# Metering TensorE's side work by a token bucket, and starting attention on the first block of keys

## The chip, the cores and the metric

One core of one Trainium2 chip. The metric is the device time of one execution of the program in microseconds (us). The kernel's time is a median of several runs, and one execution is also profiled: its trace is what the text reads. The core's engines are TensorE (PE in the profile: matmuls, with weight loads shown apart as PEld), VectorE (DVE), ScalarE (ACT), GpSimd (POOL) and SyncE (SP). Each runs its own queue of instructions in the order written; they meet at semaphores.

## The reference

Two equal layers over x of 2048 tokens by 512, in bfloat16, and each layer does two steps:

```python
x = x + A(layernorm(x))     # attention: 32 heads of 16, all 2048 keys, no mask
x = x + B(layernorm(x))     # (gelu(x @ w_gate) * (x @ w_up)) @ w_down, 1792 wide

def A(x):
    q, k, v = split(x @ wqkv)                       # each 32 heads x 2048 x 16
    p = softmax(q @ k.T * 16 ** -0.5)
    return merge_heads(p @ v) @ wo
```

Both layers use the same weights. The layer norm has no scale and no shift.

## The kernel before

All activations stay on the chip. `X` holds the residual as 16 tiles of 128 tokens in float32; `XNT` holds the normalised x, transposed; `KT` the keys, `VP` the values with a column of ones, `WQM` the query weights spread out so that four heads fill the array's row groups with zeros between.

**Slots.** The attention of a layer is cut into 32 units: four blocks of 512 queries (`qb`) times eight groups of four heads (`g`). A unit has 32 slots: 16 tiles of 128 keys (`kt`) times two pairs of heads (`hp`). A slot (`a_slot`) is two score matmuls on TensorE side by side (line 608), and one exponential of 128 x 1024 on ScalarE (line 613). Both layers together have 2048 slots. The scores go round three pairs of PSUM banks, so TensorE can be up to two slots ahead of ScalarE. After a lag of three slots the second slot of a pair is followed by `pv` (line 626): four matmuls side by side that add into bank 7. At the end of a unit VectorE copies bank 7 out (line 453), and after four units the sums' reciprocals are sent through DRAM and multiplied in on GpSimd (line 437, `AT`).

**Side work.** Everything else that TensorE does is put between slots by a planner written in Python; its decisions fix each engine's order of instructions. There are two sources. `prep` is a list of projections with gates: keys and values of each pair of head groups (`kproj`, `vproj`; lines 343 and 358 copy them out) and the query of each unit (`qproj`, copied out by line 337). `posts` holds a generator per block of queries (`post`): it waits for the block's last unit, then gives the four out-projections (into `X`, line 473), the layer norm (`ln_tiles`: statistics on VectorE, lines 284 and 285; scaling on GpSimd, lines 289 to 295), ten slots later four transposes (`transpose_tile`, lines 308 and 312), then the gate projections with their gelus in one burst (`g_slot`, lines 577 and 583), 14 up-projections (multiplied into `HT` by line 513) and 4 x 7 pieces of the down-projection (line 521, copied out by 537 or 532). For all layers but the last it ends with the layer norm for the next layer. All this side work but the gate burst uses one PSUM bank, `misc.banks = [6]`.

Each step has a nominal cost: 216 ns for a matmul of 512 columns, so 864 for a query, key or up-projection, 1024 for values, 1728 for an out-projection, 432 for a piece of the down-projection, 224 for a transposed tile. In every slot, side work is given out as long as the sum spent in that slot is under `BUDGET`, 520. So one projection, or two pieces of the down-projection, go into every slot while there is any.

`force` makes a missing query, key or value at once; where its block has not yet passed through `post`, it drains `posts`, with seven PSUM banks. That happens at the layer boundary: in slot 24 of layer two, whose keys of block 3 need the end of layer one's block 3. The post of the last block runs after the last slot in the same way.

**Head.** Loads of `X` go out from GpSimd's queue in four pieces of 512 tokens (issued at 1.3, 2.3, 3.1 and 3.8 us), converted to float32 on the way; weights go out from SP's queue: the keys', queries' and values', then, after ScalarE has cleared `WOP`, eight pieces of wo, then gate, up and down. VectorE clears `WQM` and spreads the query weights into it (8 copies, line 263). GpSimd clears and fills some tiles (lines 253 to 278). Then, for each of the four blocks: layer norm, four transposes; after block 0 also its keys, the first query and its values. The slots begin after the fourth block.

The planner's loop before the change:

```python
spent = 0.0
...                                   # slot: force q and k, a_slot, run_pv, flush_norm
while spent < BUDGET:
    c = prep_try()
    if c is None:
        break
    spent += c
while spent < BUDGET and posts:
    c = next(posts[0], "end")
    ...
    spent += c
```

Of the kernel before, what the change touches and what calls it, by code (L numbers as in the profile page):

```python
# [9 lines left out]
ALU = mybir.AluOpType  # L10
ACTF = mybir.ActivationFunctionType
# [140 lines left out]
def _emit_fast(nc, es, x_in, wqkv, wo, wg, wu, wd, out, n_rep=2):  # L152
# [5 lines left out]
    NCK = D // 128  # L158
    NG = 2 * NCK
    NFT = F // 128  # L160
    NTT = S // 128
    NQB = S // 512
# [62 lines left out]
    class Ring:  # L225
# [4 lines left out]
        def next(self):  # L230
            self.pos += 1
            return self.banks[self.pos % len(self.banks)]
# [3 lines left out]
    def dma(eng, grp, dst, src, r=(), w=(), serial=False):  # L236
        if grp not in sch.groups:
            sch.add_dma_group(grp, serial=serial)
        sch.op(eng, lambda e: e.dma_start(dst, src), r=r, w=w, grp=grp)  # L239

    def pe(fn, r, w):
        sch.op("pe", fn, r=r, w=w)


    wq_src = wqkv.rearrange("(a p) n -> p a n", p=128)
    for b in range(NQB):
        dma("pool", "ldx%d" % b, X[:, 4 * b:4 * b + 4, :],
            x_in[0, 512 * b:512 * (b + 1), :].rearrange("(a p) c -> p a c", p=128),
            w=[("X", 4 * b + i) for i in range(4)])
# [5 lines left out]
    sch.op("pool", lambda e: e.affine_select(IDN[:], ONB[:], [[1, 128]], ALU.is_equal, 0.0,  # L255
                                              base=0, channel_multiplier=-1),
           r=[("ONB",)], w=[("IDN",)])
    sch.op("dve", lambda e: e.memzero(WQM[:].rearrange("p a b c -> p (a b c)")), w=[("WQM",)])
    for c in range(NCK):
        for p in range(2):  # L260
            dst = AP(WQM, (2 * c + p) * 128 + 16 * p, [[NCK * NG * 128, 128], [NG * 128, NCK], [32, 4], [1, 16]])
            src = AP(HT, 128 * c + 16 * p, [[NFT * 512, 128], [D, NCK], [32, 4], [1, 16]])
            sch.op("dve", lambda e, dst=dst, src=src: e.tensor_copy(dst, src), r=HTALL + [("WQM",)], w=[("WQM",)])
    sch.op("dve", lambda e: e.memset(PS[:, 7, :], 0.0), w=[BK[7]])
    sch.op("act", lambda e: e.memzero(WOP[:].rearrange("p a b -> p (a b)")), w=[("WOP", j, p) for j in range(4) for p in range(2)])
    for j in range(4):
        for p in range(2):
            src = AP(wo.tensor, wo.offset + (32 * j + 16 * p) * D, [[D, 16], [128 * D, NCK], [1, D]])
            dst = AP(WOP, 32 * j * NG * D + p * D, [[NG * D, 16], [2 * D, NCK], [1, D]])
            dma("sp", "ldw_o%d%d" % (j, p), dst, src, w=[("WOP", j, p)])  # L270
    dma("sp", "ldw_g", WG[:], wg.rearrange("(a p) n -> p a n", p=128), w=[("WG",)])
    dma("sp", "ldw_u", WU[:], wu.rearrange("(a p) n -> p a n", p=128), w=[("WU",)])
    dma("sp", "ldw_d", WD[:], wd.rearrange("(a p) n -> p a n", p=128), w=[("WD",)])
    sch.op("pool", lambda e: e.memset(AP(VP, 16, [[NKT * H * VW, 128], [VW, NKT * H]]), 1.0), w=[("VPONE",)])
    sch.op("pool", lambda e: e.memset(RB[:], 0.0), w=[("RB", i, j) for i in range(2) for j in range(4)])
    sch.op("pool", lambda e: e.memset(OKL[:], 1.0), w=[("OKL",)])
# [1 line left out]
    sch.op("pool", lambda e: e.memset(LT[:], 1.0), w=[("LT", i, j) for i in range(HB) for j in range(4)])  # L278


    def ln_tiles(tts, check=False):
        n = len(tts)
        for i, tt in enumerate(tts):
            sch.op("dve", lambda e, i=i, tt=tt: e.bn_stats(ST[:, i, :], X[:, tt, :]), r=[("X", tt)], w=[("ST", i)])
            sch.op("dve", lambda e, i=i: e.bn_aggr(MV[:, i, :], ST[:, i, :]), r=[("ST", i)], w=[("MV", i)])
        mvk = [("MV", i) for i in range(n)]
        mean = AP(MV, 0, [[8, 128], [2, n]])
        var = AP(MV, 1, [[8, 128], [2, n]])
        sch.op("pool", lambda e: e.tensor_scalar(LNS[:, 0, 0:n], var, LN_EPS, None, op0=ALU.add), r=mvk, w=[("LNS",)])
        sch.op("pool", lambda e: e.tensor_tensor(LNS[:, 1, 0:n], LNS[:, 0, 0:n], CM05[:, 0:n], op=ALU.pow),  # L290
               r=[("LNS",), ("CM05",)], w=[("LNS",)])
        sch.op("pool", lambda e: e.tensor_scalar(LNS[:, 2, 0:n], mean, -1.0, None, op0=ALU.mult),
               r=mvk + [("LNS",)], w=[("LNS",)])
        for i, tt in enumerate(tts):
            sch.op("pool", lambda e, i=i, tt=tt: e.tensor_scalar(  # L295
                XN[:, i, :], X[:, tt, :], LNS[:, 2, i:i + 1], LNS[:, 1, i:i + 1], op0=ALU.add, op1=ALU.mult),
                r=[("X", tt), ("LNS",)], w=[("XN", i)])
# [5 lines left out]
    def transpose_tile(i, tt):  # L303
        b = misc.next()

        def fn(e):
            for ck in range(NCK):
                ins = e.transpose(bankbf(b)[:, ck * 128:(ck + 1) * 128], XN[:, i, ck * 128:(ck + 1) * 128], IDN[:, :])  # L308
            return ins

        pe(fn, [("XN", i), ("IDN",)], [BK[b]])
        sch.op("dve", lambda e: e.tensor_copy(XNT[:, :, tt * 128:(tt + 1) * 128],  # L312
                                              bankbf(b)[:, 0:NCK * 128].rearrange("p (a b) -> p a b", a=NCK)),
               r=[BK[b]], w=[("XNT", tt)])
        return 56.0 * NCK

    def mm512(pairs, rkeys, evac, cols=512):
# [12 lines left out]
    def xk(b):  # L330
        return [("XNT", 4 * b + i) for i in range(4)]

    def qproj(u, slot):
        qb, g = u // NG, u % NG
        return mm512([(WQM[:, ck, g, :], XNT[:, ck, 512 * qb:512 * (qb + 1)]) for ck in range(NCK)],
                     xk(qb) + [("WQM",)],
                     lambda b: sch.op("dve", lambda e: e.tensor_copy(Q[:, slot, :], bank(b)),  # L337
                                      r=[BK[b]], w=[("Q", slot)]))

# [294 lines left out]
    posts = []  # L634
# [14 lines left out]
            misc.banks = [6]  # L649


    misc.banks = list(range(7))
    for b in range(NQB):
        ln_tiles([4 * b + i for i in range(4)])
        for i in range(4):
            transpose_tile(i, 4 * b + i)
        have.add(("xnt", 0, b))
        if b == 0:
            for _ in range(3):
                prep_try()  # L660
    misc.banks = [6]

    seqs = [(layer, u, kt, hp) for layer in range(n_rep) for u in range(NU) for kt in range(NKT) for hp in range(2)]
    LAG = 3
    pend = []
    nxt = 0
    BUDGET = 520.0

    def run_pv(limit):
        while pend and pend[0][0] <= limit:  # L670
# [12 lines left out]
    while nxt < len(seqs) or pend:  # L683
        step = state["step"]
        if state["gslots"] is not None and nxt < len(seqs):
            qb = state["gslots"]
            for pair in range(NFT // 2):
                g_slot(qb, pair)
            state["gslots"] = None
        spent = 0.0  # L690
# [12 lines left out]
        flush_norm(step)  # L703
        while spent < BUDGET:
            c = prep_try()
            if c is None:
                break
            spent += c
        while spent < BUDGET and posts:
            c = next(posts[0], "end")  # L710
            if c == "end":
                posts.pop(0)
                continue
            if c is None:
                break
            spent += c
        state["step"] += 1
    flush_norm()
    misc.banks = list(range(7))
# [862 lines left out]
```

## Time and profile before

| | us |
|---|---|
| median of 3 runs (2504.36 to 2505.81) | 2504.52 |
| the profiled execution | 2506.37 |
| its span, first to last instruction | 2504.6 |
| ScalarE busy | 1993.2 |
| TensorE matmuls busy | 2159.2 |
| start of the first exponential | 52.74 |
| granted TensorE clock, mean of the span | 0.659 |

In the profile's rows an instruction group has its line, engine, operation, tile written and tiles read, shape and count, then busy time, mean ns of one, and the idle time of its engine before it with what ended that. In a timeline a row gives start and length in us, and in square brackets the idle time before it with what ended it. A row of windows gives the stretch, its length, and for each engine the busy time with the count of instructions; then the granted TensorE clock (1.00 is full), the share of DMA and GB/s. A matmul's end is modelled, so the distance between starts is the better measure.

### The profile page before, as it was taken

How to read it: one execution, taken by the hardware profiler on the slowest of the kernel's cores; microseconds unless marked ns; L12 is line 12 of the kernel's file. 1: busy time of each engine (PE TensorE's matmuls, PEld its weight loads, DVE VectorE, ACT ScalarE, POOL GpSimd, SP SyncE). 2: the span in 40 equal slices, each digit the busy share in tenths (PEclk: the TensorE clock that was granted, in tenths of full speed). 3: DMA queues.
4: the chain of work that ended last, by engine and by line, in shares of the span. 5: the costliest groups of instructions: out<-in, count | busy, mean ns of one | idle time of the engine just before them, and what ended most of it. 6: DMA issues, size and time to landing. Idle time of an engine off the chain costs nothing.

```text
span 2504.6 us, 25781 instructions
## 1 busy us (share of the span) xinstructions
PE 2159.2 (86%) x10945; PEld 537.1 (21%) x10945; DVE 361.0 (14%) x634; ACT 1993.2 (80%) x2121; POOL 160.9 (6%) x192
## 2 busy tenths in 40 slices
PE   3899889888889888898788888889988998889968
PEld 1321112111221112212132211221112111221113
DVE  4210012100120002100132100210012000120003
ACT  1689976999769996899727899679986899769971
POOL 4000010000100000000100000100000000100000
PEclk7855569555795558756588655785568655695558
DMA  7000000000000000000000000000000000000000
GB/s 189 1 1 10 1 10 1 1 10 1 10 1 10 1 10 1 1 10 1 10 1 1 1 10 4 7 9 10 1 10 3 7 10 1 10 9 6 5 10 10
DMA packets 21147, 25.07 MB, mean 10 GB/s; under 512 B 5920, under 2 KB 13856, under 8 KB 21024
## 3 DMA queue, kind: packets, MB, share of 16 engines
q1 hardware_dynamic: 18912, 19.16, 3.0%
q0 software_dynamic: 2112, 4.19, 0.6%
q8 instruction: 87, 1.43, 0.2%
q14 instruction: 36, 0.29, 0.0%
HBM read 18.09 MB, written 2.62 MB: 8 GB/s over the span
## 4 chain that ended last, share of the span: by engine, by line
ACT 54%; PE 31%; DVE 8%; DMA 3%; POOL 2%; SPq 2%; issue 1%; POOLq 0%; DVEq 0%
ACT fPT L613 54%; PE fPS L323 13%; PE fPS L577 4%; PE fPS L521 4%; PE fPS L608 4%; DVE fHT L513 2%; PE fPS L626 2%; SPq L239 2%; PE fPS L353 2%; DMA fRB<-rscr 1%; PE fPS L308 1%; POOL fXN L295 1%; POOL fAT L437 1%; DVE fVP L358 1%; DVE fKT L343 1%
## 5 line engine op out<-in xcount | busy, mean ns | idle before, releaser
L613 ACT ACTIVATE fPT<-fPS 128x1024 bf16<-128x1024 f32 x2048 | 1913.4, 1184 | 390.8 <-PE fPS L608 389.3
L608 PE MATMUL fPS<-fQ,fKT 32*128 32x512 bf16 x4096 | 1102.1, 553 | 172.5 <-ACT fPT L613 163.4
L626 PE MATMUL fPS<-fPT,fVP 128*17 128x512 bf16 x4096 | 573.1, 550 | 1.4 <-ACT fPT L613 1.4
L608 PEld LDWEIGHTS fPS<-fQ,fKT 32*128 32x128 bf16 x4096 | 198.7, 97 | 1064.0 <-ACT fPT L613 984.9
L453 DVE COPY fOS<-fPS 128x512 f32<-128x512 f32 x64 | 44.3, 692 | 1361.6 <-PE fPS L626 1361.6
L437 POOL TENSOR_TENSOR fAT<-fOS,fRB 128x512 bf16<-128x512 f32 x64 | 81.0, 1265 | 1874.9 <-DMA fRB<-rscr 1874.9
L626 PEld LDWEIGHTS fPS<-fPT,fVP 128*17 128x17 bf16 x4096 | 101.1, 90 | 400.0 <-issue 395.8
L323 PE MATMUL fPS<-fXNT,fWU 128*128 128x512 bf16 x448 | 111.6, 381 | 23.2 <-DVE fHT L513 18.1
L583 ACT ACTIVATE fHT<-fPS 128x1024 bf16<-128x1024 f32 x56 | 57.4, 1024 | 92.3 <-PE fPS L577 92.3
L521 PE MATMUL fPS<-fWD,fHT 128*128 128x512 bf16 x448 | 113.7, 381 | 13.1 <-DVE fXN L532 4.7
L323 PE MATMUL fPS<-fXNT,fWQM 128*128 128x512 bf16 x256 | 111.8, 587 | 4.3 <-DVE fX L537 1.4
L577 PE MATMUL fPS<-fXNT,fWG 128*128 128x512 bf16 x448 | 110.4, 412 | 0.8 <-DVE fXNT L312 0.5
L513 DVE TENSOR_TENSOR fHT<-fPS,fHT 128x512 bf16<-128x512 f32 x112 | 77.5, 692 | 216.5 <-PE fPS L323 216.3
L323 PE MATMUL fPS<-fWOP,fAT 128*128 128x512 bf16 x256 | 74.8, 447 | 37.5 <-POOL fAT L437 31.3
L308 PE MATMUL fPS<-fIDN,fXN 128*128 128x128 bf16 x256 | 38.9, 307 | 70.1 <-POOL fXN L295 56.3
L577 PEld LDWEIGHTS fPS<-fXNT,fWG 128*128 128x128 bf16 x448 | 46.3, 105 | 63.9 <-issue 18.8
L337 DVE CAST fQ<-fPS 128x512 bf16<-128x512 f32 x64 | 44.3, 692 | 71.0 <-PE fPS L323 71.0
L323 PEld LDWEIGHTS fPS<-fXNT,fWU 128*128 128x128 bf16 x448 | 37.0, 98 | 80.6 <-DVE fHT L513 46.1
L521 PEld LDWEIGHTS fPS<-fWD,fHT 128*128 128x128 bf16 x448 | 36.0, 98 | 69.1 <-issue 16.3
L323 PE MATMUL fPS<-fXNT,fWK 128*128 128x512 bf16 x128 | 40.3, 446 | 9.8 <-DVE fVP L358 5.9
L295 POOL TENSOR_SCALAR fXN<-fX,fLNS 128x512 bf16<-128x512 f32 x64 | 48.3, 770 | 1.7
L473 DVE TENSOR_TENSOR fX<-fPS,fX 128x512 f32<-128x512 f32 x32 | 22.1, 692 | 181.3 <-PE fPS L323 181.3
(45 smaller groups left out, 391.0 us busy)
## 6 DMA issues: line engine op xcount, KB each, us to landing
fRB<-rscr SPq DMA_DIRECT2D x256, 32.0 KB, 1.8
fX<-in_A_x_dram POOLq DMA_DIRECT2D x4, 1024.0 KB, 17.2
fLT<-fOS SPq DMA_DIRECT2D x256, 2.0 KB
out_dram<-fXN SPq DMA_DIRECT2D x16, 128.0 KB, 1.7
fWG<-in_B_w_gate_dram SPq DMA_DIRECT2D x1, 1792.0 KB, 19.3
fWU<-in_B_w_up_dram SPq DMA_DIRECT2D x1, 1792.0 KB, 24.6
fWD<-in_B_w_down_dram SPq DMA_DIRECT2D x1, 1792.0 KB, 29.2
fWK<-in_A_wqkv_dram SPq DMA_DIRECT2D x1, 512.0 KB, 4.3
```

The lines of the kernel that those rows point to most:

```text
L239: sch.op(eng, lambda e: e.dma_start(dst, src), r=r, w=w, grp=grp)
L295: sch.op("pool", lambda e, i=i, tt=tt: e.tensor_scalar(XN[:, i, :], X[:, tt, :], LNS[:, 2, i:i + 1], LNS[:, 1, i:i + 1], op0=ALU.add, op1= ...
L308: ins = e.transpose(bankbf(b)[:, ck * 128:(ck + 1) * 128], XN[:, i, ck * 128:(ck + 1) * 128], IDN[:, :])
L323: ins = e.matmul(bank(b)[:, 0:cols], lhsT=l, rhs=r_, start=(i == 0), stop=(i == n - 1))
L437: sch.op("pool", lambda e, g=g, slot=slot, os_=os_: e.tensor_tensor(AT[:, g, :], OS[:, os_, :], RB[:, slot, :], op=ALU.mult), r=[("OS", os ...
L513: lambda b, ft=ft: sch.op("dve", lambda e: e.tensor_tensor(HT[:, ft, :], bank(b), HT[:, ft, :], op=ALU.mult), r=[BK[b], ("HT", ft)], w=[(" ...
L521: ins = e.matmul(bank(b)[:, 0:D], lhsT=HT[:, ft, i * 128:(i + 1) * 128], rhs=WD[:, ft, :], start=(ft == 0), stop=(ft == NFT - 1))
L577: ins = e.matmul(bank(2 * s + jj), lhsT=WG[:, ck, ft * 128:(ft + 1) * 128], rhs=XNT[:, ck, xs], start=(ck == 0), stop=(ck == NCK - 1))
L583: sch.op("act", lambda e: e.activation(HT[:, 2 * pair:2 * pair + 2, :], PS[:, 2 * s:2 * s + 2, :], ACTF.Gelu_apprx_tanh), r=bks, w=[("HT", ...
L608: ins = e.matmul(bank(2 * s + jj), lhsT=KT[32 * j:32 * j + 32, c, kt * 128:(kt + 1) * 128], rhs=Q[32 * j:32 * j + 32, qs, :], start=True, ...
L613: sch.op("act", lambda e: e.activation(PT[:, p, :].rearrange("p (a b) -> p a b", a=2), PS[:, 2 * s:2 * s + 2, :], ACTF.Exp, scale=SCALE), ...
L626: ins = e.matmul(PS[32 * j:32 * j + VW, 7, :], lhsT=VP[:, kt, h, :], rhs=PT[:, ps[j // 2], (j % 2) * 512:(j % 2 + 1) * 512], start=(kt == ...
```

## The change

- **Bucket.** A slot no longer has a budget of its own. Tokens are added at 420 a slot up to 600, and side work is given out while the tokens are above zero, so that a costly piece is paid back in the slots after it.
- **Head.** Block 0 of `X` is loaded in four tiles. Before the first slot only block 0 is normalised and transposed (copied out by ScalarE instead of VectorE) and its keys and the first query made; block 1's layer norm stands before that in VectorE's and GpSimd's queues. A generator, `head`, is put first into `posts`: it gives the transposes of blocks 1, 2 and 3 from slots 5, 13 and 21 on, each after the layer norm of the next block. Odd blocks are normalised into `AT`, which is free then, instead of `XN`.
- **Setup.** Clearing `WQM` and spreading it go from VectorE to ScalarE, clearing `WOP` from ScalarE to GpSimd. Each part of `WQM` has a key of its own. The loads of gate, up and down wait until all of `X` has landed.

```diff
-    for b in range(NQB):
+    for t in range(4):
+        dma("pool", "ldx0_%d" % t, X[:, t, :], x_in[0, 128 * t:128 * (t + 1), :], w=[("X", t)])
+    for b in range(1, NQB):
         dma("pool", "ldx%d" % b, X[:, 4 * b:4 * b + 4, :],
...
-    sch.op("dve", lambda e: e.memzero(WQM[:].rearrange("p a b c -> p (a b c)")), w=[("WQM",)])
+    sch.op("act", lambda e: e.memzero(WQM[:].rearrange("p a b c -> p (a b c)")), w=[("WQM",)])
...
-            sch.op("dve", lambda e, dst=dst, src=src: e.tensor_copy(dst, src), r=HTALL + [("WQM",)], w=[("WQM",)])
+            sch.op("act", lambda e, dst=dst, src=src: e.activation(dst, src, ACTF.Copy), r=HTALL + [("WQM",)],
+                   w=[("WQMx", c, p)])
...
-    sch.op("act", lambda e: e.memzero(WOP[:].rearrange("p a b -> p (a b)")), w=[...])
+    sch.op("pool", lambda e: e.memzero(WOP[:].rearrange("p a b -> p (a b)")), w=[...])
...
-    dma("sp", "ldw_g", WG[:], wg.rearrange("(a p) n -> p a n", p=128), w=[("WG",)])
+    dma("sp", "ldw_g", WG[:], wg.rearrange("(a p) n -> p a n", p=128), r=[("X", NTT - 1)], w=[("WG",)])
...                                                    # the same for ldw_u and ldw_d
+        if eng == "act":
+            sch.op("act", lambda e: e.activation(dst, src, ACTF.Copy), r=[BK[b]], w=[("XNT", tt)])
+        else:
+            sch.op("dve", lambda e: e.tensor_copy(dst, src), r=[BK[b]], w=[("XNT", tt)])
...
+    def head():
+        def ln(b):
+            ln_tiles([4 * b + i for i in range(4)], alt=bool(b % 2) and NG >= 4)
+
+        ln(0)
+        for b in range(NQB):
+            if b + 1 < NQB:
+                ln(b + 1)
+            for i in range(4):
+                transpose_tile(i, 4 * b + i, alt=bool(b % 2) and NG >= 4, eng="act" if b == 0 else "dve")
+            have.add(("xnt", 0, b))
+            yield None
+            while not state["drain"] and state["step"] < 8 * b + 5:
+                yield None
+
+    posts.append(head())
     misc.banks = list(range(7))
-    for b in range(NQB):
-        ln_tiles([4 * b + i for i in range(4)])
-        for i in range(4):
-            transpose_tile(i, 4 * b + i)
-        have.add(("xnt", 0, b))
-        if b == 0:
-            for _ in range(3):
-                prep_try()
+    next(posts[0])
+    prep_try()
+    prep_try()
     misc.banks = [6]
...
-    BUDGET = 520.0
+    RATE, CAP = 420.0, 600.0
+    tokens = 0.0
...
-        while spent < BUDGET:
+        tokens = min(CAP, tokens + RATE)
+        while tokens > 0:
             c = prep_try()
             if c is None:
                 break
-            spent += c
-        while spent < BUDGET and posts:
+            tokens -= c
+        while tokens > 0 and posts:
             c = next(posts[0], "end")
...
-            spent += c
+            tokens -= c
```

More of the change, by code (lines that the diff above doesn't have):

```diff
@@ L262, in _emit_fast @@
             src = AP(HT, 128 * c + 16 * p, [[NFT * 512, 128], [D, NCK], [32, 4], [1, 16]])
-            sch.op("dve", lambda e, dst=dst, src=src: e.tensor_copy(dst, src), r=HTALL + [("WQM",)], w=[("WQM",)])
+            sch.op("act", lambda e, dst=dst, src=src: e.activation(dst, src, ACTF.Copy), r=HTALL + [("WQM",)],
+                   w=[("WQMx", c, p)])
     sch.op("dve", lambda e: e.memset(PS[:, 7, :], 0.0), w=[BK[7]])
-    sch.op("act", lambda e: e.memzero(WOP[:].rearrange("p a b -> p (a b)")), w=[("WOP", j, p) for j in range(4) for p in range(2)])
+    sch.op("pool", lambda e: e.memzero(WOP[:].rearrange("p a b -> p (a b)")), w=[("WOP", j, p) for j in range(4) for p in range(2)])
     for j in range(4):
@@ L270, in _emit_fast @@
             dma("sp", "ldw_o%d%d" % (j, p), dst, src, w=[("WOP", j, p)])
-    dma("sp", "ldw_g", WG[:], wg.rearrange("(a p) n -> p a n", p=128), w=[("WG",)])
-    dma("sp", "ldw_u", WU[:], wu.rearrange("(a p) n -> p a n", p=128), w=[("WU",)])
-    dma("sp", "ldw_d", WD[:], wd.rearrange("(a p) n -> p a n", p=128), w=[("WD",)])
+    dma("sp", "ldw_g", WG[:], wg.rearrange("(a p) n -> p a n", p=128), r=[("X", NTT - 1)], w=[("WG",)])
+    dma("sp", "ldw_u", WU[:], wu.rearrange("(a p) n -> p a n", p=128), r=[("X", NTT - 1)], w=[("WU",)])
+    dma("sp", "ldw_d", WD[:], wd.rearrange("(a p) n -> p a n", p=128), r=[("X", NTT - 1)], w=[("WD",)])
     sch.op("pool", lambda e: e.memset(AP(VP, 16, [[NKT * H * VW, 128], [VW, NKT * H]]), 1.0), w=[("VPONE",)])
@@ L278, in _emit_fast, with xn, xnkey, ln_tiles @@
     sch.op("pool", lambda e: e.memset(LT[:], 1.0), w=[("LT", i, j) for i in range(HB) for j in range(4)])
-    def ln_tiles(tts, check=False):
+    def xn(i, alt):
+        return AT[:, i, :] if alt else XN[:, i, :]
+    def xnkey(i, alt):
+        return ("AT", i) if alt else ("XN", i)
+    def ln_tiles(tts, check=False, alt=False):
         n = len(tts)
@@ L295, in ln_tiles @@
             sch.op("pool", lambda e, i=i, tt=tt: e.tensor_scalar(
-                XN[:, i, :], X[:, tt, :], LNS[:, 2, i:i + 1], LNS[:, 1, i:i + 1], op0=ALU.add, op1=ALU.mult),
-                r=[("X", tt), ("LNS",)], w=[("XN", i)])
+                xn(i, alt), X[:, tt, :], LNS[:, 2, i:i + 1], LNS[:, 1, i:i + 1], op0=ALU.add, op1=ALU.mult),
+                r=[("X", tt), ("LNS",)], w=[xnkey(i, alt)])
         if check:
@@ L301, in ln_tiles, with transpose_tile @@
                    r=mvk + [("OKV",)], w=[("OKV",)])
-    def transpose_tile(i, tt):
+    def transpose_tile(i, tt, alt=False, eng="dve"):
         b = misc.next()
@@ L307, in fn @@
             for ck in range(NCK):
-                ins = e.transpose(bankbf(b)[:, ck * 128:(ck + 1) * 128], XN[:, i, ck * 128:(ck + 1) * 128], IDN[:, :])
+                ins = e.transpose(bankbf(b)[:, ck * 128:(ck + 1) * 128], xn(i, alt)[:, ck * 128:(ck + 1) * 128], IDN[:, :])
             return ins
[L311 to L314, printed above, removed]
+        pe(fn, [xnkey(i, alt), ("IDN",)], [BK[b]])
+        dst = XNT[:, :, tt * 128:(tt + 1) * 128]
+        src = bankbf(b)[:, 0:NCK * 128].rearrange("p (a b) -> p a b", a=NCK)
+        if eng == "act":
+            sch.op("act", lambda e: e.activation(dst, src, ACTF.Copy), r=[BK[b]], w=[("XNT", tt)])
+        else:
+            sch.op("dve", lambda e: e.tensor_copy(dst, src), r=[BK[b]], w=[("XNT", tt)])
         return 56.0 * NCK
@@ L335, in qproj @@
         return mm512([(WQM[:, ck, g, :], XNT[:, ck, 512 * qb:512 * (qb + 1)]) for ck in range(NCK)],
-                     xk(qb) + [("WQM",)],
+                     xk(qb) + [("WQMx", g // 2, g % 2)],
                      lambda b: sch.op("dve", lambda e: e.tensor_copy(Q[:, slot, :], bank(b)),
@@ L689, in _emit_fast @@
             state["gslots"] = None
-        spent = 0.0
         if nxt < len(seqs):
```

## The prediction

> **What bounds the kernel now.** I read the page's first table, then the chain of waits and the costliest groups.
>
> ```profile
> span 2504.6 us, 25781 instructions
> PE 2159.2 (86%) x10945; PEld 537.1 (21%) x10945; DVE 361.0 (14%) x634; ACT 1993.2 (80%) x2121; POOL 160.9 (6%) x192
> ...
> ACT 54%; PE 31%; DVE 8%; DMA 3%; POOL 2%; SPq 2%; issue 1%; POOLq 0%; DVEq 0%
> ...
> L613 ACT ACTIVATE fPT<-fPS 128x1024 bf16<-128x1024 f32 x2048 | 1913.4, 1184 | 390.8 <-PE fPS L608 389.3
> ```
>
> The chain lies on ScalarE (ACT) for 54%: the 2048 exponentials of line 613. Before them ACT is idle 390.8 us, nearly all of it waiting for the scores of line 608. Where nothing but attention runs, ACT does not wait; the timeline of a unit without side work gives its pace, and windows cut at the starts of exponentials show the pace with side work beside it.
>
> ```profile
> 52.74 1.02 ACT L613 ACTIVATE fPT<-fPS 128x1024 bf16<-128x1024 f32 x1 [48.75 <-PE fPS L608]
> ...
> 2047.41 17.52 ACT L613 ACTIVATE fPT<-fPS 128x1024 bf16<-128x1024 f32 x19 [0.85 <-PE fPS L608]
> ...
> core 0: us, PE busy (x) PEld busy (x) DVE busy (x) ACT busy (x) POOL busy (x), PEclk, DMA share, GB/s
> 394.28:417.33 23.05, 19.36 (x102) 5.70 (x100) 8.62 (x13) 14.12 (x14) 0.00 (x0) 1.00 0.00 1
> 417.33:440.32 22.99, 20.81 (x112) 6.15 (x112) 3.46 (x6) 14.34 (x14) 0.00 (x0) 1.00 0.00 1
> ...
> sum 276.23, PE 240.98 PEld 71.10 DVE 72.50 ACT 170.78 POOL 0.00; mean PE 20.08 PEld 5.92 DVE 6.04 ACT 14.23 POOL 0.00
> ...
> 52.74:83.11 30.37, 25.53 (x208) 11.90 (x207) 10.72 (x16) 16.39 (x16) 0.00 (x0) 0.93 0.00 1
> ...
> 1118.51:1122.25 3.74, 3.54 (x18) 0.84 (x18) 0.84 (x2) 2.05 (x2) 0.00 (x0) 0.50 0.03 6
> ...
> sum 137.99, PE 118.73 PEld 54.13 DVE 46.77 ACT 74.12 POOL 0.00; mean PE 16.96 PEld 7.73 DVE 6.68 ACT 10.59 POOL 0.00
> ...
> ...
> sum 80.06, PE 66.89 PEld 22.36 DVE 14.38 ACT 25.74 POOL 5.79; mean PE 11.15 PEld 3.73 DVE 2.40 ACT 4.29 POOL 0.97
> ...
> 1242.38:1306.18 63.80, 47.41 (x218) 20.89 (x218) 24.04 (x47) 10.76 (x10) 9.06 (x14) 0.84 0.00 0
> ```
>
> Undisturbed, nineteen exponentials take 17.52 us, and a single one lasts 1.02 (the first at 52.74), so they follow each other every (17.52 − 1.02) / 18 = 0.917 us. What a stretch takes beyond 0.917 us a slot I call its excess. The up-projection of one block is 14 slots in 23.05 us, 10.2 us of excess; the down-projection is 14 slots in 22.99. Six blocks run so beside attention; their twelve stretches (the first two shown, then the sum) are 168 slots in 276.23 us, an excess of 122 us, 61 each. The seven stretches of key and value projections (first and fourth shown, then their sum) hold 73 slots in 137.99 us: 71 us. The out-projections, four slots in each of six blocks, take 80.06 us (the sum shown): 58 us. The other costs, the head, the gate bursts, the layer boundary and the tail, have other causes. So 251 us are lost because a side unit (four full matmuls, 864 ns by the planner) goes into every slot.
>
> Why a slot with a unit takes 1.83 us is in the timeline of an up-projection and of a down-projection:
>
> ```profile
> 409.72 0.69 DVE L513 TENSOR_TENSOR fHT<-fPS,fHT 128x512 bf16<-128x512 f32 x1 [1.13 <-PE fPS L323]
> 410.47 1.04 PE L323 MATMUL fPS<-fXNT,fWU 128*128 128x512 bf16 x4 [0.47 <-DVE fHT L513]
> 411.44 0.39 PE L608 MATMUL fPS<-fQ,fKT 32*128 32x512 bf16 x2
> ...
> 434.84 0.60 PE L521 MATMUL fPS<-fWD,fHT 128*128 128x512 bf16 x2 [0.79 <-DVE fX L537]
> 435.37 0.39 PE L608 MATMUL fPS<-fQ,fKT 32*128 32x512 bf16 x2
> 435.69 0.39 PE L626 MATMUL fPS<-fPT,fVP 128*17 128x512 bf16 x4
> 436.02 1.04 PE L521 MATMUL fPS<-fWD,fHT 128*128 128x512 bf16 x4
> ```
>
> The unit holds TensorE 0.97 us (410.47 to 411.44), then VectorE empties the only side bank (0.69 us), and the next unit, with the next scores behind it in TensorE's queue, waits for that (0.47). At full clock one slot's scores take 0.32 us (435.37 to 435.69), a pair's PV 0.33, or 0.16 a slot, and two down matmuls 0.53 (434.84 to 435.37). At half clock the same steps are:
>
> ```profile
> 337.27 0.60 PE L608 MATMUL fPS<-fQ,fKT 32*128 32x512 bf16 x2 [0.52 <-ACT fPT L613]
> 337.80 0.61 PE L626 MATMUL fPS<-fPT,fVP 128*17 128x512 bf16 x4
> 338.34 0.60 PE L608 MATMUL fPS<-fQ,fKT 32*128 32x512 bf16 x2
> ...
> 370.23 1.89 PE L323 MATMUL fPS<-fXNT,fWQM 128*128 128x512 bf16 x4
> 372.05 0.61 PE L608 MATMUL fPS<-fQ,fKT 32*128 32x512 bf16 x2
> ```
>
> Scores 0.53, PV 0.27 a slot, a unit 1.82.
>
> **The change, part by part.** *The bucket.* It adds 420 a slot, so a unit of 864 goes out every 864 / 420 = 2.06 slots and a down piece of 432 nearly every slot; work beyond that slips to later slots. A block's side work by the planner's costs, 4 × 1728 + 14 × 864 + 28 × 432 + 8 × 224 = 32,896, then needs 78 slots (at 420) instead of 38 (at 864), of the 256 that a block lasts, so nothing is late but at the layer boundary (below).
>
> Up-projection: TensorE needs 2.06 × 0.48 + 0.97 = 1.96 us a unit, ACT 2.06 × 0.917 = 1.89. TensorE binds by 0.07 us; scores run up to two slots ahead, which evens out the lumps. 84 units × 0.07 = 6; I take 8 instead of 61 (bounds 0 and 61): −53 us.
>
> Down-projection: 1.03 × 0.48 + 0.53 = 1.02 against 0.94, 0.08 for each of 168 pieces, 13 us; at each of 24 tile changes the next piece waits for VectorE, 0.79 less the scores and PV now between, 0.3, 7 us. 20 instead of 61 (bounds 7 and 61): −41 us.
>
> Keys and values: 62 units. These bursts begin at half clock, where a unit costs 2.06 × 0.80 + 1.82 − 1.89 = 1.58 us. I let two units of each of six bursts run so (19 us) and 50 at 0.1: 24 instead of 71 (bounds 5 and 98): −47 us.
>
> Out-projection (eight matmuls, 1728, so every 4.1 slots): at full clock 1.90 + 4.1 × 0.48 = 3.87 against 3.76, next to nothing; at half 3.57 + 4.1 × 0.80 − 3.76 = 3.1. The first of each block stays at half clock and waits for POOL's normalised tile (2.09):
>
> ```profile
> 349.67 3.57 PE L323 MATMUL fPS<-fWOP,fAT 128*128 128x512 bf16 x8 [2.09 <-POOL fAT L437]
> 356.71 1.90 PE L323 MATMUL fPS<-fWOP,fAT 128*128 128x512 bf16 x8
> ```
>
> That is 5.2 a block and nearly nothing for the rest: 32 instead of 58 (bounds 13 and 87): −26 us.
>
> Q projections lie mostly in attention without other side work, one a unit, and stay; some fall into the longer metered stretches: −5 (bounds 0 and −12). The gate bursts are emitted whole, as before: 0. At the layer boundary slot 24 of the next layer forces what is left; two out-projections that ran in slots then fall into that drain, and pay about what they paid: 0.
>
> *The head.*
>
> ```profile
> 6.99 1.25 POOL L275 MEMSET fRB<- 128x1024 f32 x1
> 14.31 0.24 POOL L289 TENSOR_SCALAR fLNS<-fMV 128x4 f32<-128x4 f32 x1 [5.75 <-DVE fMV L285]
> 23.36 0.69 DVE L337 CAST fQ<-fPS 128x512 bf16<-128x512 f32 x1 [0.41 <-PE fPS L323]
> ...
> DMA to landing us min/median/max: 9.0/17.2/26.8
> ```
>
> Block 0's query is cast by 24.05; the first exponential starts at 52.74, as its row showed, because three more blocks are normalised and transposed first. After the change it could start 0.65 us behind the cast, at 24.7. POOL's setup gets longer: the WOP clearing (twice RB's columns, 2.5 us) and three more DMA issues (0 to 2.4) move its end from 8.56 (14.31 less the 5.75 of waiting) to between 11.1 and 13.5, still ahead of 14.31; VectorE loses the WQM copies to ACT, which is idle, and starts its statistics when the tiles land, by 10.3 (issue at 1.3 plus 9.0). So 14.31 moves up by 1.6 or so: first exponential at 23.2. The casts of K and Q now stand behind block 1's statistics on VectorE; were its rows to land 17.2 us after an issue at 2.3, plus 3.4 us of statistics, it would be 25.4 (the other end). −29.5 us.
>
> What it costs: the transposes of blocks 1 to 3 now stand in front of scores, on one side bank: four at 1.12 us (374.03 after 372.90 in the next rows) make 4.5 us, less the two slots' lead. Three of them left ACT idle 2.62 us here. Block by block 3 us, +9 (bounds 3 and 14).
>
> ```profile
> 372.90 0.61 PE L308 MATMUL fPS<-fIDN,fXN 128*128 128x128 bf16 x4 [0.25 <-DVE fQ L337]
> 374.03 0.61 PE L308 MATMUL fPS<-fIDN,fXN 128*128 128x128 bf16 x4 [0.52 <-DVE fXNT L312]
> ...
> 376.34 1.02 ACT L613 ACTIVATE fPT<-fPS 128x1024 bf16<-128x1024 f32 x1 [2.62 <-PE fPS L608]
> ```
>
> The gate, up and down weights now wait on SP for all of X; nothing else stands there until the first unit ends, and they are first read some 270 us on: 0.
>
> Sum: −53 − 41 − 47 − 26 − 5 − 29.5 + 9 = −192.5. The profiled execution took 2506.37 around its span of 2504.6; against the median of 2504.52 I get 2312.
>
> **Does the clock hold?** This decides most. Windows of 3.4 us around a Q projection, and in an up-projection:
>
> ```profile
> 268.30:271.70 3.40, 3.27 (x14) 0.74 (x14) 0.96 (x2) 2.82 (x4) 0.00 (x0) 0.50 0.00 1
> 271.70:275.10 3.40, 2.20 (x20) 0.57 (x16) 0.42 (x1) 3.15 (x4) 0.00 (x0) 0.99 0.01 2
> 275.10:278.50 3.40, 2.96 (x16) 0.50 (x14) 0.00 (x0) 3.40 (x5) 0.00 (x0) 0.51 0.00 0
> ...
> 402.00:405.40 3.40, 2.79 (x16) 0.81 (x15) 1.38 (x2) 1.85 (x2) 0.00 (x0) 1.00 0.00 0
> ```
>
> One unit lifts the granted clock for the next window; a window of attention alone drops it, although TensorE reads busy for 2.96 of its 3.40 us. Metered, a unit comes each 1.9 us instead of each 1.83 and the scores between double, so a window holds as much dense work as the one at 402, which stayed at 1.00. In the row at 410.47 TensorE idled 0.47 us before the unit, and the clock stayed full. The Trainium skill ("TensorE: Matmul & The Clock Gate", section "A second HAM failure mode: psum-queue depth-cycling") speaks against the change: short idle times between groups of matmuls, it says, make the clock swing between half and full. The trace does not agree so far, by that 0.47.
>
> **The rivals.** *Clock lost* (slower): thinned work does not keep the clock. All at half is U 133, D 168 × 0.79 = 133, K and V 98, out-projection 87: 451 where the sum has 84, +367, 2679. It decides from 192.5 / 367 = 52% of the metered work at half clock. For it: attention alone runs at 0.50. Against: the window at 402. 0.04.
>
> *Clock swings*: half of the metered work at half clock, by the idle times that the wider spacing leaves between units: +183, 2495. For it: the clock changes from one 3.4 us window to the next around 271.70. Against: the row at 410.47 and 23 us of up-projection at 1.00. 0.04. This is the skill's section named above.
>
> *Half clock where a burst starts cold*: keys, values and out-projections never lift it, up and down, behind the gate burst, do: +74 + 55, 2441. For it: the two projections at 1118.51 ran at 0.50 throughout. 0.10.
>
> *TensorE is the bound anyway* (the change doesn't do what it says): spread or not, each unit costs the same, and only the head is won, 2484. For it: PE reads 86% busy. Against: 0.48 + 0.97 us of need in a slot of 1.83. 0.04.
>
> *All of it hides*: U 0, D 7, K and V 5, out-projection 13, so 59 less, 2253. 0.13.
>
> **How the numbers follow.** Forecast 0.63, its own range 2280 to 2360; 0.02 for what I do not see. The range takes in the hidden case and the lower part of the cold-burst case: 2250 to 2400, about 0.8. A change of 0.2% (5 us) is about what can be told from none. Faster 0.63 + 0.13 + 0.10 + 0.04 + 0.04 = 0.94, same 0.02, slower 0.04.
>
> **What would show it.** Right: first exponential at 23 to 25.5 us; up-projection units in about 29 slots of some 28 us at clock 1.00; down pieces at about 1.02 us a slot; line 613's idle time down from 390.8 to some 200. Wrong: PEclk below 0.8 in those stretches, exponentials 1.3 us or more apart beside side work, or a drain at the boundary (the row at 1242.38) much over 63.8 us.

## The result, and the profile after

The changed kernel takes 2275.31 us (median of 4 runs, 2274.16 to 2277.6) against 2505.16 for the kernel before in the same session: a ratio of 0.9084, interval 0.9068 to 0.9099. The forecast was 2312 in a range of 2250 to 2400. The time fell by 230 us where 192.5 were forecast, and half of the difference stands in one term of the sum, the queries.

The page of the changed kernel, beside the lines shown of the one before (the exponentials are line 625 now, the scores 620):

```profile
span 2274.6 us, 25800 instructions
PE 2003.7 (88%) x10945; PEld 518.6 (23%) x10945; DVE 353.9 (16%) x621; ACT 1981.6 (87%) x2133; POOL 164.0 (7%) x196
...
ACT 54%; PE 33%; DVE 5%; DMA 3%; POOL 2%; SPq 2%; issue 1%; POOLq 0%; DVEq 0%
...
L625 ACT ACTIVATE fPT<-fPS 128x1024 bf16<-128x1024 f32 x2048 | 1896.9, 1192 | 157.5 <-PE fPS L620 153.2
```

ScalarE's busy time hardly moved (1993.2 to 1981.6); its waiting before exponentials fell from 390.8 to 157.5 us, which is the difference between the two spans, 230.0 us, to within a few us.

Windows of the same stages, cut at starts of exponentials: an up-projection (29 slots), a down-projection (31), the sum of all twelve such stretches, and the drain at the layer boundary. Then ScalarE's timeline at the head and in an up-projection:

```profile
352.73:379.58 26.85, 25.47 (x174) 7.80 (x174) 10.02 (x16) 26.85 (x30) 0.00 (x0) 1.00 0.00 1
380.50:411.78 31.28, 30.39 (x187) 7.76 (x186) 3.78 (x6) 29.53 (x32) 0.00 (x0) 1.00 0.01 1
...
sum 348.78, PE 335.17 PEld 93.35 DVE 82.78 ACT 338.24 POOL 0.00; mean PE 27.93 PEld 7.78 DVE 6.90 ACT 28.19 POOL 0.00
...
1110.36:1177.65 67.29, 51.32 (x233) 22.36 (x231) 25.05 (x48) 10.76 (x11) 9.06 (x14) 0.85 0.00 0
...
22.75 1.02 ACT L625 ACTIVATE fPT<-fPS 128x1024 bf16<-128x1024 f32 x1 [4.82 <-PE fPS L620]
...
359.07 9.62 ACT L625 ACTIVATE fPT<-fPS 128x1024 bf16<-128x1024 f32 x10
```

In the up-projection ScalarE is busy for all of its 26.85 us: 14 side units now lie beside 29 exponentials without a wait, at clock 1.00. The twelve stretches hold 360 slots in 348.78 us, 18.7 us over 0.917 a slot; before they held 168 slots and 122 us of excess. The first exponential starts at 22.75.

To sort all the excess, I put each interval between the starts of two exponentials down to the side work that stands between their scores in TensorE's queue, less 0.917 us:

| term, us | before | after | difference | forecast |
|---|---|---|---|---|
| first exponential | 52.7 | 22.7 | −30 | −29.5 |
| transposes of blocks 1 to 3 among the slots | 0 | 6.3 | +6 | +9 |
| up-projection, 84 units | 61.3 | 1.3 | −60 | −53 |
| down-projection, 168 pieces | 60.9 | 14.0 | −47 | −41 |
| keys and values | 65.5 | 19.4 | −46 | −47 |
| out-projections, with the boundary's | 68.5 | 40.6 | −28 | −26 |
| queries | 76.7 | 52.5 | −24 | −5 |
| gate bursts, other transposes, pure slots, tail | | | −1 | 0 |

(After, 3.5 us of the out-projections' 40.6 are the longer drain: two of them joined it. Beside attention they cost 37.0.)

### The profile page after: what moved, and what is told of

Its sections match the earlier page's. It is cut to its first block, busy times and chain, and to the rows that moved or that the text cites. A ratio compares the mean times of both kernels' runs of the same rounds, so it can differ in the third digit from the quotient of the medians.

```text
span 2274.6 us, 25800 instructions
## 1 busy us (share of the span) xinstructions
PE 2003.7 (88%) x10945; PEld 518.6 (23%) x10945; DVE 353.9 (16%) x621; ACT 1981.6 (87%) x2133; POOL 164.0 (7%) x196
## 3 DMA queue, kind: packets, MB, share of 16 engines
q0 software_dynamic: 2160, 4.19, 0.8%
## 4 chain that ended last, share of the span: by engine, by line
ACT 54%; PE 33%; DVE 5%; DMA 3%; POOL 2%; SPq 2%; issue 1%; POOLq 0%; DVEq 0%
ACT fPT L625 54%; PE fPS L335 11%; PE fPS L620 7%; PE fPS L533 5%; PE fPS L589 5%; PE fPS L638 4%; SPq L239 2%; DVE fHT L525 1%; DMA fRB<-rscr 1%; PE fPS L317 1%; POOL fAT L449 1%; DMA rscr<-fRT 1%; DMA fLT<-fOS 1%; DVE fXNT L326 1%; DVE fQ L349 1%
## 5 line engine op out<-in xcount | busy, mean ns | idle before, releaser
L625 ACT ACTIVATE fPT<-fPS 128x1024 bf16<-128x1024 f32 x2048 | 1896.9, 1192 | 157.5 <-PE fPS L620 153.2
L620 PE MATMUL fPS<-fQ,fKT 32*128 32x512 bf16 x4096 | 997.1, 518 | 159.4 <-ACT fPT L625 149.8
L638 PE MATMUL fPS<-fPT,fVP 128*17 128x512 bf16 x4096 | 536.7, 514 | 4.5 <-DVE fOS L465 2.8
L620 PEld LDWEIGHTS fPS<-fQ,fKT 32*128 32x128 bf16 x4096 | 189.7, 96 | 965.9 <-ACT fPT L625 840.5
L533 PE MATMUL fPS<-fWD,fHT 128*128 128x512 bf16 x448 | 126.2, 383 | 5.3 <-DVE fX L549 1.4
L335 PE MATMUL fPS<-fXNT,fWQM 128*128 128x512 bf16 x256 | 98.7, 527 | 0.9
L317 PE MATMUL fPS<-fIDN,fXN 128*128 128x128 bf16 x224 | 33.6, 304 | 47.0 <-POOL fXN L304 34.4
L293 DVE BATCH_NORM_STATS2 fST<-fX 128x6 f32<-128x512 f32 x64 | 42.7, 667 | 8.3 <-DMA fX<-in_A_x_dram 8.3
L533 PEld LDWEIGHTS fPS<-fWD,fHT 128*128 128x128 bf16 x448 | 30.1, 97 | 58.2 <-issue 32.7
L335 PEld LDWEIGHTS fPS<-fWOP,fAT 128*128 128x128 bf16 x256 | 25.9, 110 | 73.7 <-issue 35.1
```

What stands on the lines that cost most here:

```text
L317: ins = e.transpose(bankbf(b)[:, ck * 128:(ck + 1) * 128], xn(i, alt)[:, ck * 128:(ck + 1) * 128], IDN[:, :])
L335: ins = e.matmul(bank(b)[:, 0:cols], lhsT=l, rhs=r_, start=(i == 0), stop=(i == n - 1))
L533: ins = e.matmul(bank(b)[:, 0:D], lhsT=HT[:, ft, i * 128:(i + 1) * 128], rhs=WD[:, ft, :], start=(ft == 0), stop=(ft == NFT - 1))
L620: ins = e.matmul(bank(2 * s + jj), lhsT=KT[32 * j:32 * j + 32, c, kt * 128:(kt + 1) * 128], rhs=Q[32 * j:32 * j + 32, qs, :], start=True, ...
L625: sch.op("act", lambda e: e.activation(PT[:, p, :].rearrange("p (a b) -> p a b", a=2), PS[:, 2 * s:2 * s + 2, :], ACTF.Exp, scale=SCALE), ...
L638: ins = e.matmul(PS[32 * j:32 * j + VW, 7, :], lhsT=VP[:, kt, h, :], rhs=PT[:, ps[j // 2], (j % 2) * 512:(j % 2 + 1) * 512], start=(kt == ...
```

## The experiments

All are edits of the changed kernel unless said. "Before" was run beside each on the same chip.

**Each half alone.** The first keeps the head, loads and setup of before, the second the old rule:

```diff
 # first: kernel before
-    BUDGET = 520.0
+    RATE, CAP = 420.0, 600.0          # and the loop over tokens
 # second: kernel after
-        while tokens > 0:
+        while spent < BUDGET:          # 520, spent = 0 in each slot
```

> The bucket alone: the head, the loads and the setup of before, the planner's token bucket of after. Main theory (the bucket keeps ScalarE fed because a side unit fits beside two slots at full clock; the head is a separate gain of 30 us less what its transposes cost): first exponential at 52.7 us as before, up-projection stretches of 29 slots in about 26.9 us, time 2295 us (2285 to 2305), that is some 20 us more than the full change. Rival (much of the gain comes from the first slots, where the new head puts key and value work into a cold clock and so warms it): the time would be under 2280 or over 2315.

> The head, loads and setup of after with the old budget of 520 a slot. Main theory: first exponential at 22.7 us, three blocks' transposes in the slots, all later stages as before: up-projection 14 slots in 23.05 us; 2485 us (2478 to 2492). Together the two halves' gains (about 20 here and 210 for the bucket) add up to the 230 of the full change. Rival (the halves help each other): the sum of the two gains misses 230 by more than 10 us.

Measured: the bucket alone 2290.79 us, ratio 0.9144 (0.9128 to 0.916); the head alone 2483.5, ratio 0.9918 (0.9901 to 0.9935). ScalarE's timeline of the two at the first exponential:

```profile
53.70 1.02 ACT L613 ACTIVATE fPT<-fPS 128x1024 bf16<-128x1024 f32 x1 [49.70 <-PE fPS L608]
```

```profile
23.26 1.02 ACT L625 ACTIVATE fPT<-fPS 128x1024 bf16<-128x1024 f32 x1 [5.09 <-PE fPS L620]
```

Against 2504.41 the gains are 213.6 and 20.9, together 234.5, next to the 230 of both: they add. The bucket is nine tenths of the change. The head starts the exponentials 29.5 us earlier and gains 20.9: some 9 go back, 6.3 of them in the transposes of blocks 1 to 3.

**The rate.** One number changed, `RATE`:

```diff
-    RATE, CAP = 420.0, 600.0
+    RATE, CAP = 260.0, 600.0           # and 600.0, and 210.0
```

> The change with 260 tokens a slot instead of 420: a unit every 3.3 slots (3.0 us), a down piece every 1.7, an out-projection every 6.6 slots (6.1 us). Main theory (the granted clock is set window by window of 3.4 us; a window with at least half its time filled by matmuls keeps full clock): behind the gate burst up- and down-projection stay at 1.00 although thinner, with no excess at all (down 2.9 to under 1 us a block); out-projections now lie further apart than a window, so each runs at half clock and costs 2 to 3 us, 7 to 10 us a block instead of 5; 2290 us (2265 to 2320). Rival (thinned work loses the clock, the rate of 420 is just dense enough): up-projection at about 0.5, its units 1.3 us of excess each, time over 2370. Second rival (clock does not matter, only TensorE's slack): everything improves, 2250.

> The change with 600 tokens a slot: a unit every 1.44 slots. Main theory (TensorE needs 0.48 a slot and 0.97 a unit at full clock, so 1.66 us against 1.32 of ScalarE): the excess returns as a TensorE bound, 0.34 a unit and 0.2 a down piece, less about 1.5 us a stretch that the two slots of lead cover: up 3 us a block, down 5 to 6, keys and values 15 in all; 2320 us (2305 to 2340), clock 1.00 in the stretches. Rival (the single side bank's round trip of 1.83 us binds rather than TensorE): down pieces, which need the bank only once in seven, would not get slower, while units at 1.44 slots would each cost 0.5 us; up 7 us a block, down unchanged at 2.9, 2330 us.

> The change with 210 tokens a slot: a unit every 4.1 slots (3.8 us), an out-projection every 8.2 (7.5 us). Main theory (the clock is set per window of 3.4 us, and a window about half filled with matmuls keeps it full): between two units 2.8 us pass, so every window still holds some 0.6 us of a unit beside the scores, and up- and down-projection stay at 1.00 with no excess; between out-projections 5.7 us pass, so two windows in three fall empty and the next one starts at half clock: 10 us or more a block where 260 tokens had 6; keys and values that start cold lift the clock more slowly. 2265 us (2245 to 2300), slower than with 260. Rival (thinner is always better, the clock does not enter): 2225 us.

Measured: 600 gives 2372.84 us, ratio 0.9474 (0.9458 to 0.949); 420 is the change, 0.9084; 260 gives 2237.98, ratio 0.8945 (0.8926 to 0.8964); 210 gives 2296.69, ratio 0.9152 (0.9136 to 0.9169). So there is a best rate, and 420 is not it. The up-projection of one block at 600 and two steps of TensorE's timeline in it, then the out-, up- and down-projection at 260, then two out-projections and the up-projection at 210:

```profile
358.59:381.97 23.38, 20.81 (x124) 6.28 (x122) 8.63 (x13) 18.46 (x19) 0.00 (x0) 1.00 0.00 1
...
380.57 1.04 PE L335 MATMUL fPS<-fXNT,fWU 128*128 128x512 bf16 x4 [0.47 <-DVE fHT L525]
381.54 0.39 PE L620 MATMUL fPS<-fQ,fKT 32*128 32x512 bf16 x2
```

```profile
299.07:326.26 27.19, 22.54 (x124) 6.62 (x124) 3.78 (x6) 20.70 (x23) 1.26 (x1) 0.78 0.01 1
362.19:406.54 44.35, 37.72 (x252) 11.36 (x250) 11.69 (x17) 44.35 (x49) 0.00 (x0) 1.00 0.00 1
408.35:453.91 45.56, 41.62 (x260) 10.54 (x260) 6.21 (x10) 45.56 (x51) 5.07 (x4) 1.00 0.05 14
...
307.05 1.90 PE L335 MATMUL fPS<-fWOP,fAT 128*128 128x512 bf16 x8
323.17 2.73 PE L335 MATMUL fPS<-fWOP,fAT 128*128 128x512 bf16 x8
```

```profile
316.99 3.60 PE L335 MATMUL fPS<-fWOP,fAT 128*128 128x512 bf16 x8
331.61 3.59 PE L335 MATMUL fPS<-fWOP,fAT 128*128 128x512 bf16 x8
...
388.70:439.95 51.25, 42.18 (x274) 12.12 (x274) 10.31 (x16) 50.83 (x56) 0.00 (x0) 0.97 0.00 1
```

At 600, 19 slots take 23.38 us, 6.0 of excess a block, and the down-projection has 7.4. Theory and rival each had one half: TensorE's need makes down pieces slower, and where two units fall into neighbouring slots the side bank's round trip (the wait of 0.47) is back. 2320 was too low because it had only the first, and because 46 queries ran at half clock: all queries cost 68 us where 420 tokens had 52.5. Keys and values cost 43 where I had 15; how much of that is the bank's round trip I did not separate.

At 260 the two projections have no excess (49 slots in 44.35 us, ScalarE busy throughout) and the clock stays at 1.00 with a unit every 3.0 us: the rival "clock lost" is refuted there. My 2290 was too high: I let most out-projections fall to half clock, and 16 of 25 held (1.90 us for eight matmuls at 307.05; 3.57 is half clock, and the 2.73 at 323.17 began at half and ended at full); the queries gained 13 us more. The time is nearest to the second rival's 2250, but that the clock does not matter is not what the trace shows: nine out-projections wholly or partly at half clock cost 36 us, 27 queries 35. At 210 the out-projections do fall (3.60 and 3.59): 23 of the 25 beside attention ran at half clock, some of them in part, and all cost 74.5 us where 260 had 36.5 (this profiled execution, 2310.16 us, is 13 above the run's median). Of the 84 up-projections 77 still hold. So thinning is not free: below some density the clock goes, and it went first for the work that lies furthest apart.

**The clock itself.** Matmuls with all-zero weights, which add nothing to the PV bank, in a pair of slots whose last side work lies at least two slots back:

```diff
+    ZER = sb("fZER", [128, 128], BF)         # zeroed by GpSimd
...
+        warm = 2 if kt > 0 and state["step"] - state["side"] >= 2 else 0
         def fn(e):
+            for _ in range(warm):
+                e.matmul(PS[:, 7, :], lhsT=ZER[:, :], rhs=WK[:, 0, 0:512], start=False, stop=False, ...)
             for j in range(4):        # PV
...
+            state["side"] = step      # wherever the planner gives side work
```

> The change as it is, plus two matmuls of 128x512 with all-zero weights, added into the PV bank ahead of a pair's PV whenever no side work was given in the last two slots; the result is the same. Main theory (what is left of the excess is mostly the price of half clock): the granted clock stays at 1.00 through all of attention, the queries that ran at half clock (37 at 1.3 us) cost next to nothing, the first out-projections only their wait for POOL (2.5 us a block instead of 5), cold keys and values 2 instead of 18 us, the gate bursts 1.5 us less each: 2175 us (2160 to 2200). Rival (the zeros' time on TensorE comes on top, or zeros do not lift the clock): 2275 to 2330 us with a clock as before.

> 260 tokens a slot and the zero matmuls. Main theory: as in the run before, from 2238: queries 40 to 5 us of excess, out-projections 36 to 15, keys and values 14 to 2, gate bursts 5 less: 2160 us (2145 to 2185). Rival (260 tokens won by keeping the clock up, so the two remedies cure the same thing): no better than the run with 420 tokens and zeros.

Measured: with 420 tokens 2254.07 us, ratio 0.8986 (0.897 to 0.9003); with 260 2210.97, ratio 0.8826 (0.8808 to 0.8844). Three lines show what the clock does to the query projections: the group of their matmuls before the change, after it, and with 420 tokens and zeros (587, 527 and 386 ns a matmul). The clock of that last run and three steps of its TensorE stand beside the third.

```profile
L323 PE MATMUL fPS<-fXNT,fWQM 128*128 128x512 bf16 x256 | 111.8, 587 | 4.3 <-DVE fX L537 1.4 <-DVE fXN L532 1.4 <-DVE fVP L358 0.7
```

```profile
L335 PE MATMUL fPS<-fXNT,fWQM 128*128 128x512 bf16 x256 | 98.7, 527 | 0.9
```

```profile
PEclk9999999999999999999889999999999999999978
...
L337 PE MATMUL fPS<-fXNT,fWQM 128*128 128x512 bf16 x256 | 67.2, 386 | 0.8
...
306.33 1.90 PE L337 MATMUL fPS<-fWOP,fAT 128*128 128x512 bf16 x8
309.14 0.60 PE L641 MATMUL fPS<-fWK,fZER 128*128 128x512 bf16 x2
310.32 1.90 PE L337 MATMUL fPS<-fWOP,fAT 128*128 128x512 bf16 x8
```

With the zeros the clock's mean over the span is 0.972, 0.702 without, no query runs at half clock, and the queries' excess falls from 52.5 to 16.6 us. But the run missed 2175 by 79: the zeros stood between units too. Two out-projections that followed each other every 3.66 us without zeros (308.26 and 311.92 in the changed kernel) are 3.99 us apart with them, out-projections cost 41 us beside attention instead of 37, and up-projections rose from 1.3 to 16. Both theories hold, each in its place: half clock costs, and so do the zeros where TensorE has no slack. With 260 tokens the forecast of 2160 was missed by 51 in the same way: out-projections cost 44 where I had 15, keys and values 15 where I had 2. That the two remedies cure the same thing is refuted: together they are 43 us faster than the zeros with 420.

**One wait, and one part undone.**

```diff
 # first, with 260 tokens
-        yield from delay(14)
+        yield from delay(18)
 # second, with 420
-    dma("sp", "ldw_g", ..., r=[("X", NTT - 1)], w=[("WG",)])       # and ldw_u, ldw_d
+    dma("sp", "ldw_g", ..., w=[("WG",)])
```

> 260 tokens, and the out-projections come 18 instead of 14 slots after the block's normalisation is given out. Theory: the first out-projection stands in TensorE's queue waiting 2.5 us for GpSimd's last normalised tile, with scores behind it; four slots later the tile is ready, which saves 2 us at each of seven blocks: 2225 us (2215 to 2232). Rival (the wait is covered by the two slots that TensorE is ahead): 2238 us as with 14.

> The change with one part undone: the loads of the gate, up and down weights do not wait for X any more, so they share the DMA engines with it as before. Theory (X is early enough anyway): block 1's rows land some 3 us later than the 13.2 us of the change, its statistics end by 20 us, about when the cast of the first keys starts on the same engine; blocks 2 and 3 are read after 24 and 36 us. First exponential at 22.7 to 24 us, time as the change, 2275 us (2272 to 2280). Rival (the deferral is what makes the early start possible): statistics of block 1 stand in front of the casts, first exponential at 26 us or later, 2279 to 2290.

Measured: the delay gives 2219.03 us, ratio 0.8853 (0.8837 to 0.8869), 19 us less than 260 tokens alone. The first out-projection of a block without the longer delay, and with it:

```profile
300.75 3.57 PE L335 MATMUL fPS<-fWOP,fAT 128*128 128x512 bf16 x8 [1.99 <-POOL fAT L449]
```

```profile
302.20 2.89 PE L335 MATMUL fPS<-fWOP,fAT 128*128 128x512 bf16 x8
```

The wait for GpSimd is gone, and the out-projections' excess beside attention falls from 36.5 to 18.1 us: ScalarE had paid for it. The early loads give 2276.32, ratio 0.9085 (0.907 to 0.91), the time of the change: that part does nothing here. VectorE's row of the statistics of block 1, in the changed kernel and with the early loads, shows why:

```profile
13.19 0.69 DVE L293 BATCH_NORM_STATS2 fST<-fX 128x6 f32<-128x512 f32 x1 [1.56 <-DMA fX<-in_A_x_dram]
```

```profile
13.26 0.69 DVE L293 BATCH_NORM_STATS2 fST<-fX 128x6 f32<-128x512 f32 x1 [1.57 <-DMA fX<-in_A_x_dram]
```

I had expected 3 us later. The `wo` pieces stand ahead of these loads on SP and wait for GpSimd's clearing of `WOP` (they go out from 8.34 us), so that the gate's load goes out at 12.00 even here, little more than 1 us before block 1's statistics start; in the change it goes out at 23.45.

**Put together.** 260 tokens, the delay of 18, and the zeros only from four slots, or six, after the last side work:

```diff
-        warm = 2 if kt > 0 and state["step"] - state["side"] >= 2 else 0
+        warm = 2 if kt > 0 and state["step"] - state["side"] >= 4 else 0      # second: 6
```

> 260 tokens, out-projections 18 slots after the normalisation, and the zero matmuls, but only when no side work was given for four slots (two in the earlier runs), so that they stay out of up-projections (3.3 slots apart) and of most of the recovery after an out-projection. Theory (the zeros cost where they stood between units, and half clock costs elsewhere): from 2219 us: queries 39 to 10, cold keys and values 16 to 5, out-projections 18 to 8, transposes 18 to 12: 2165 us (2150 to 2185). Rival (the zeros cost what they win): 2200 to 2220.

> As the run before with a gap of six slots, so that the zeros stay out between out-projections (6.6 slots apart) too. Theory: the clock is dropped after one window of 3.4 us (3.7 slots) without dense work, so with six slots it falls to half before the zeros lift it again; more time at half clock than with four, 2175 us (2155 to 2195), not faster than with four. Rival (the zeros' own cost is the larger one): faster than with four by 5 us or more.

Measured: four slots 2174.0 us, ratio 0.8668 (0.8653 to 0.8682); six slots 2180.92, ratio 0.87 (0.8686 to 0.8715). The first, the fastest kernel here, beats the change by 101 us. Its page:

```profile
PEclk9999999999999999999889999999999999999978
...
L627 ACT ACTIVATE fPT<-fPS 128x1024 bf16<-128x1024 f32 x2048 | 1885.9, 1291 | 78.8 <-PE fPS L622 77.9
```

ScalarE's waiting before exponentials is down to 78.8 us, of 390.8 at the start. Both times lie in the forecast ranges. Six slots were slower than four by 7 us, with a mean clock of 0.934 against 0.970, as the theory said.

## Why the prediction was right, and where it was off

- **Mechanism: right.** The up- and down-projections lost most of their excess (122 us to 18.7 in the windows), keys and values two thirds, out-projections two fifths; the bucket alone (2290.79) shows that it is the bucket that did it. That TensorE is the bound anyway (2484) is refuted.
- **Clock: right.** All twelve up- and down-projection stretches ran at 1.00. Of the "clock swings" and "cold burst" rivals only a little came true: seven key and five value projections ran at half clock, some in part, 18 us, near the 19 that the sum had. Clock swings were priced at +183 us; the metered stretches show none, and at 600 tokens, with the wait of 0.47 us before the unit at 380.57, the clock is 1.00 too. The Trainium skill ("TensorE: Matmul & The Clock Gate", section "A second HAM failure mode: psum-queue depth-cycling") describes such swings from short idle times between groups of matmuls; the trace does not agree here.
- **Up-projection: 1.3 instead of 8, and not for the sum's reason.** Behind the gate burst the scores end 2.05 us ahead of their exponential. A side unit then stands between the scores of two slots, and a pair of slots needs 1.94 us of TensorE (scores at 360.24 and 362.18 below) against ScalarE's 1.83. The lead is gone by 360, and the next three pairs pay 0.1 us each. From 368 on the unit stands behind the PV matmuls and the scores of two slots next to each other: all four matmuls take 0.33 us (368.21 to 368.54), where one slot's two take 0.32 (361.53 to 361.85). Such a pair needs 0.33 + 0.33 + 0.97 = 1.63, and nothing more is paid. The step "2.06 × 0.48" charged each slot's scores apart, and each unit where only what exceeds the lead is paid. The down-projection has a piece in nearly every slot, so that scores seldom become neighbours. It begins with 0.95 us of lead, uses that up in six slots, and paid nearly what was forecast: 14.0 for 20.
- **Queries: the term that was mis-sized.** The step read "some fall into the longer metered stretches: −5 (bounds 0 and −12)". Measured: −24, outside these bounds, of which some 5 I had counted with the keys and values. I did not count how many: a block's metered stretches grew to some 78 of its 256 slots, and with them the queries at full clock from 10 to 26 of 63. At half clock a query costs 1.3 us, at full 0.14 (3.6 us for 26). Sixteen that changed sides are 19 us. The runs agree: at 260 tokens 27 are left at half clock, at 600 there are 46, with zeros at 420 none.
- **Head: right.** 22.75 for 23.2; the transposes cost 6.3 for 9. **Boundary: off by 3.5**, two out-projections that the drain pays for in full.

```profile
360.24 0.39 PE L620 MATMUL fPS<-fQ,fKT 32*128 32x512 bf16 x2
360.56 1.04 PE L335 MATMUL fPS<-fXNT,fWU 128*128 128x512 bf16 x4
361.53 0.39 PE L620 MATMUL fPS<-fQ,fKT 32*128 32x512 bf16 x2
361.85 0.39 PE L638 MATMUL fPS<-fPT,fVP 128*17 128x512 bf16 x4
362.18 0.39 PE L620 MATMUL fPS<-fQ,fKT 32*128 32x512 bf16 x2
...
368.21 0.40 PE L620 MATMUL fPS<-fQ,fKT 32*128 32x512 bf16 x4
368.54 0.39 PE L638 MATMUL fPS<-fPT,fVP 128*17 128x512 bf16 x4
369.06 1.04 PE L335 MATMUL fPS<-fXNT,fWU 128*128 128x512 bf16 x4
```

The traces' clock records narrow down the density at which the clock goes. They change only at multiples of 3.41 us. I counted such windows in the attention of the nine traces without zeros, gate bursts left out, by the side matmuls of 512 columns that start in them (four of 128 columns count as one). At full clock, all 1483 windows with four or more were followed by full clock, and 336 of 345 with none by half clock; with one to three, 158 were followed by full and 16 by half. At half clock, none of 2650 windows with at most one was followed by full clock, and 158 of 231 with four were. So at 210 tokens a unit every 3.8 us held: the 2.8 us between two units are less than a window. Between out-projections, 5.7 us have room for a window without any.

What stays open is what decides between one and three. How much of the old 1.83 us a slot a second side bank would have cured was not tried.

## What to carry to other kernels

Where one engine paces a kernel and another has side work, give the work out at the rate of the slack, not in bursts: the same work costs next to nothing if the need in a stretch stays within the pace and the buffers between the two engines take up the lumps. Then read the TensorE clock by stage: a stage that reads 90% busy at half clock has slack that dense work would uncover, and a rate has an optimum, because too thick overruns the slack and too thin loses the clock. Count which other work comes to run at full clock when a dense stretch becomes longer.

## What the runs showed of the hardware that I had not expected

- Matmuls with all-zero weights hold the granted clock up: 0.97 over the span with them, 0.70 without (420 tokens).
- Narrow score and PV matmuls alone do not: a window of attention with two queries beside it has, in the changed kernel, TensorE busy for 56.17 of 63 us at 0.55, and a window with zeros, two queries and the start of an out-projection (260 tokens, four slots) 53.41 at 1.00, for 68 and 69 exponentials.

```profile
1300.00:1363.00 63.00, 56.17 (x278) 10.71 (x276) 2.77 (x4) 61.30 (x68) 0.00 (x0) 0.55 0.00 1
```

```profile
1300.00:1363.00 63.00, 53.41 (x343) 14.27 (x350) 4.83 (x8) 62.25 (x69) 5.07 (x4) 1.00 0.04 10
```

- Scores of two slots that stand next to each other in TensorE's queue take 0.33 us together, one slot's alone 0.32. Where side work stands decides TensorE's need, and not only how much of it there is.
